# Linear attention and a two-layer MoE: fixed-scale float16 attention products, with a range flag and a float32 path behind a branch

## The chip, the cores and the metric

The kernel runs on one core of a Trainium2 chip. Its engines are TensorE (PE, matrix products, with PEld for its weight loads), VectorE (DVE), ScalarE (ACT), GpSimd (POOL) and SyncE (SP, which issues most DMAs). Each engine works its own list of instructions in order and waits for the others by semaphores. The metric is the device time of one execution in microseconds, the median of the runs.

## The reference

Inputs: q, k, v of 8 batches, 8 heads, 576 tokens and 64 numbers; w_phi, 64 by 128; the MoE's two weights, 512 by 2048 and 2048 by 512, which come as float64. The attention is linear: every token is projected to 128 features, and the products go over features.

```python
def phi(x):
    proj = np.einsum('bhsd,df->bhsf', x, w_phi)
    proj = proj - np.max(np.abs(proj), axis=-1, keepdims=True)
    return np.concatenate([np.exp(proj), np.exp(-proj)], axis=-1)
q_p, k_p = (phi(q), phi(k))
kv = np.einsum('bhsf,bhsd->bhfd', k_p, v)
z = np.sum(k_p, axis=2)
num = np.einsum('bhsf,bhfd->bhsd', q_p, kv)
den = np.einsum('bhsf,bhf->bhs', q_p, z)[..., None] + 1e-06
# x: (num / den) as 4608 tokens by 512
h = x @ w_in
g = h * (1.0 / (1.0 + np.exp(-1.702 * h)))
return (g @ w_out).astype(np.float32)
```

The inputs are normal numbers: q, k, v and w_phi with spread 0.1, then q times 8, k times 3.368 and w_phi times 3.904; the MoE's weights with spread 1/sqrt(512) and 1/sqrt(2048).

## The kernel before

**How the list is made.** The whole program is written as operations that a `Recorder` collects. Each belongs to a part with a priority; a planner goes through them by priority, with its own costs, and writes one order for every engine. `emit` (line 399, which therefore stands in every row of the profile) then issues them. There are no loops on the chip: the program is one straight list.

**Attention.** A batch is worked in four units of two heads (`attn_unit`), with 512 tokens each in the main part and the last 64 tokens of all heads in a tail. A unit loads k, q and v (`kq`, `vn`), scales k and q by powers of two taken from their own maxima (`kq_scales`), splits them into two float16 parts (`xs`), turns them by a DMA transpose (`xT`), projects them by two float16 matmuls (`ph`), and subtracts each token's largest magnitude (DVE: `sm`, then `t`). For keys the features are Exp of +t and -t (`features_k`). For queries (`features_q`) `t` is first transposed on PE, four 128-column matmuls, since the next product needs features on the partitions. Features are split into a high part, which is a second Exp with another output type (`eh`), and a rest (`el`, `elb`, on DVE). Key features times v give `kf`, a 128 by 66 matrix for each sign and head: 64 columns of values, one that sums the features (z). After a split of `kf` (`kz`, `kzs`, `kzb`) queries times these give numerator and denominator (`nf`), and `xf` is their quotient, split again into `xo` and turned by DMA into the MoE's input `x`. The first batch and one more unit work in plain float32 (`project_whole`, `exact`).

**MoE.** The weights stay on the chip, each as two float16 parts (`wbuf`), after a scale found from their squares (`weight_scales`, `wsq`) and a split (`split_weights`). Chunks of 384 token columns run over 16 blocks of 128 hidden features: `hb` collects three float16 products (high by high, high by rest, rest by high) for each quarter of the 512 inputs, ACT makes `th` by tanh, DVE makes `g` from it, ACT and DVE split it into `gh` and `gl`, and three products of 512 columns go into `ab`. The first 512 columns go in two halves of the weights, so that work can begin before all weights are there. Attention of later batches is spread between MoE chunks by the priorities; the last part of the program is MoE alone.

**Number types on PE.** A float32 matmul is two records in the profile (a transpose is one), a float16 one is one.

## Time and profile before

| | |
|---|---|
| median of 3 runs | 1081.18 us (1080.14 to 1081.76) |
| span of the profiled execution | 1079.0 us |
| PE, DVE, ACT, POOL busy | 1046.1, 851.1, 713.4, 247.1 us |
| instructions | 22925 |
| MoE alone at the end | from about 905 us of the span |
| HBM read, written | 54.59 MB, 9.44 MB |

A row of a group gives line, engine, operation, output<-input, partitions by elements, type and count, then busy time and the mean of one in ns, then idle time before it and what ended it. A row of the timeline starts with the start and the length in us. A row of a stretch gives its bounds and length, then for PE, PEld, DVE, ACT and POOL the busy time with the count, then the granted TensorE clock, the DMA share and GB/s. Means of groups include waiting inside the pipeline, so that operations in a row take less time each than their mean.

### The profile page before, as it was taken

What the parts mean: (1) busy time and instruction counts of PE and PEld (TensorE: products, weight loads), DVE (VectorE), ACT (ScalarE), POOL (GpSimd) and SP (SyncE); (2) the same over time, 40 slices, a digit from 0 to 9 for tenths busy, and PEclk for the clock granted to TensorE, in tenths of its full rate; (3) what the DMA queues carried; (4) which work ended last, traced back from release to release, by engine and by line L of the source; (5) the groups of instructions that cost most, each with busy time, mean ns of one, the idle gap of its engine ahead of it and who ended that gap; (6) DMA issues with size and microseconds to landing.
All of it is one profiled execution on the core that took longest, in us unless ns stands there. A gap on an engine that the chain in (4) does not pass through costs nothing.

```text
span 1079.0 us, 22925 instructions
## 1 busy us (share of the span) xinstructions
PE 1046.1 (97%) x8943; PEld 723.7 (67%) x8943; DVE 851.1 (79%) x1772; ACT 713.4 (66%) x1488; POOL 247.1 (23%) x320
## 2 busy tenths in 40 slices
PE   5998999999999999999999999999999999999997
PEld 3665677778766666678866666677876666577653
DVE  5879999999999997987899978987889675232323
ACT  4778797777878686875786676866687665332322
POOL 5666113331122213211223113111133112000000
PEclk9998999999999999999999999999999999999999
DMA  8956233434343443331244342432232110000101
GB/s 277 301 186 173 87 88 70 100 76 97 76 97 94 114 98 72 82 89 31 62 126 112 57 84 50 94 84 36 56 73 60 31 40 20 1 31 2 30 1 30
DMA packets 177452, 88.59 MB, mean 82 GB/s; under 512 B 143424, under 2 KB 168128, under 8 KB 177088
## 3 DMA queue, kind: packets, MB, share of 16 engines
q1 hardware_dynamic: 177184, 86.87, 32.5%
q8 instruction: 70, 1.15, 0.4%
q10 hardware_dynamic: 160, 0.26, 0.1%
q14 instruction: 38, 0.31, 0.1%
HBM read 54.59 MB, written 9.44 MB: 59 GB/s over the span
## 4 chain that ended last, share of the span: by engine, by line
PE 76%; DVE 13%; ACT 5%; issue 3%; DMA 1%; SPq 1%; POOL 0%; DVEq 0%; ACTq 0%; POOLq 0%
PE ab L399 30%; PE hb L399 29%; PE at L399 17%; DVE sm L399 2%; DVE wbuf L399 2%; DVE gl L399 1%; DVE t L399 1%; ACT e L399 1%; DVE ks L399 1%; DVE el L399 1%; DVE xs L399 1%; DVE elb L399 1%; DVE g L399 1%; SPq L399 1%; DVE vs L399 1%
## 5 line engine op out<-in xcount | busy, mean ns | idle before, releaser
L399 PE MATMUL hb<-x,wbuf 128*128 128x192 f16 (+3 forms) x3264 | 476.4, 280 | 1.2 <-DVE g L399 0.6
L399 PEld LDWEIGHTS <-wbuf 128*128 128x128 f16 (+1 forms) x3392 | 286.4, 98 | 79.9 <-issue 1.8
L399 PE MATMUL ab<-wbuf,gh 128*128 128x512 f16 x1152 | 337.9, 380 | 0.5 <-ACT gh L399 0.3
L399 ACT ACTIVATE th<-hb,usc 128x384 f32<-128x384 f32 (+1 forms) x208 | 115.8, 558 | 145.5 <-PE hb L399 142.8
L399 PE MATMUL ab<-wbuf,gl 128*128 128x512 f16 x576 | 194.1, 379 | 1.4 <-DVE gl L399 1.1
L399 DVE SCALAR_TENSOR_TENSOR g<-th,hb 128x384 f32<-128x384 f32 (+1 forms) x208 | 107.1, 516 | 95.6 <-ACT th L399 93.3
L399 PEld LDWEIGHTS <-gh 128*128 128x128 f16 x1152 | 107.7, 98 | 81.1 <-ACT gh L399 2.6
L399 ACT ACTIVATE gh<-g,al 128x384 f16<-128x384 f32 (+1 forms) x176 | 106.9, 607 | 52.6 <-DVE g L399 52.0
L399 DVE SCALAR_TENSOR_TENSOR gl<-g,al,gh 128x384 f16<-128x384 f32 (+1 forms) x176 | 109.9, 625 | 39.9 <-ACT gh L399 31.4
L399 POOL TENSOR_TENSOR xf<-nf,rc 128x512 f32<-128x512 f32 x28 | 34.2, 1220 | 410.8 <-DVE rc L399 331.3
L399 PE MATMUL at<-ph,xT 128*128 128x128 f16 x976 | 102.4, 219 | 0.0
L399 DVE TENSOR_REDUCE sm<-at 128x4 f32<-128x512 f32 x126 | 85.6, 680 | 17.8 <-PE at L399 17.4
L399 ACT ACTIVATE e<-at 128x512 f32<-128x512 f32 x144 | 85.4, 601 | 20.8 <-PE at L399 19.7
L399 ACT ACTIVATE e<-t 128x512 f32<-128x512 f32 x144 | 88.2, 630 | 11.8 <-DVE t L399 11.1
L399 DVE SCALAR_TENSOR_TENSOR t<-at,ks,sm 128x512 f32<-128x512 f32 x122 | 90.4, 743 | 1.1
L399 PEld LDWEIGHTS <-gl 128*128 128x128 f16 x576 | 54.8, 98 | 50.4 <-DVE gl L399 8.9
L399 DVE TENSOR_TENSOR el<-e,eh 128x512 f16<-128x512 f32 x108 | 75.4, 698 | 13.3 <-ACT eh L399 11.5
L399 DVE TENSOR_TENSOR elb<-e,eh 128x512 bf16<-128x512 f32 x110 | 77.9, 708 | 5.7 <-ACT eh L399 4.3
L399 PE MATMUL at<-vs,eh 128*128 128x132 f32 x216 | 81.8, 379 | 0.0
L399 PE MATMUL at<-kzs,eh 128*128 128x132 f32 x224 | 79.4, 373 | 0.8 <-ACT nf L399 0.5
L399 PEld LDWEIGHTS <-xT 128*128 128x128 f16 x976 | 69.8, 98 | 12.9 <-issue 0.3
L399 ACT ACTIVATE eh<-t 128x512 fp32r<-128x512 f32 x109 | 67.1, 635 | 1.1 <-DVE t L399 1.1
(199 smaller groups left out, 1845.6 us busy)
## 6 DMA issues: line engine op xcount, KB each, us to landing
vn<-in_v_dram SPq DMA_DIRECT2D x64, 128.0 KB, 2.7
kq<-in_k_dram SPq DMA_DIRECT2D x32, 256.0 KB, 3.2
kq<-in_q_dram SPq DMA_DIRECT2D x32, 256.0 KB, 3.0
tl<-in_v_dram SPq DMA_DIRECT2D x18, 384.0 KB, 3.2
x<-in_moe_w_in_dram SPq DMA_DIRECT2D x10, 512.0 KB, 6.0
x<-in_moe_w_out_dram SPq DMA_DIRECT2D x10, 512.0 KB, 6.3
out_dram<-osb SPq DMA_DIRECT2D x36, 128.0 KB, 2.4
out_dram<-osb SPq DMA_DIRECT2D x16, 256.0 KB, 2.5
```

The lines of the kernel that those rows point to most:

```text
L399: f(*[g(a) for a in args], **{k: g(a) for k, a in kw.items()})
```

## The change

**The fast path** (`attn_moe_fast`) takes fixed powers of two for all scales in place of maxima: `kq_scales`, `batch_max`, `weight_scales` and `split_weights` go. All attention products use float16 high and rest parts; `el` is always float16. The high part is a copy of the float32 Exp and no longer a second Exp. Copies, scalings and two-input operations may be given by the planner to one of two or three engines (`R.evac`: ACT or DVE, `R.two`: DVE or POOL, `R.three`: all), whichever is free first. The projection of queries is done twice, once by token for the maximum alone and once with features on the partitions, by two 512-column matmuls (`project_q`), in place of `t` and its transposes; the maximum then enters as a factor (`token_scales`). Only keys of batch 0 are in plain float32 (`EXK`), and batch 0 runs in phases: all keys, then the queries of half of the tokens, then of the other half.

**The flag** (`in_range`) compares the largest magnitudes of v, the weights and w_phi with bounds (`lo_hi`), the sums `akz` with 1e30 and every entry of `art` with 16. `numden` with `more` puts z, summed over all 128 features, into a column of `nt`, and `ratio` adds z times the reciprocal of the denominator (`rc`) to `art`, unit by unit. The flag is the smallest of all conditions.

**The branch.** All engines load the flag; where it is 0, `attn_moe_general` computes everything again in float32 into the same output: a loop over batches with 8 heads in its body, tiles of 96 tokens, the weights in float32, and a second loop over batches for the MoE with 6 tiles in its body.

```diff
-    def parts(b, src, e, hi, lo):
-        his, los = two(hi, b, "eh"), two(lo, b, "el")
-        for i, sg in enumerate((1.0, -1.0)):
-            R.scalar.activation(e[i], src, AF.Exp, scale=sg)
-            R.scalar.activation(his[i], src, AF.Exp, scale=sg)
-            h = his[i] if i == 0 and b else f32(his[i])
-            R.vector.tensor_sub(los[i], e[i], h)
-        return list(zip(his, los))
...
-        qt = psa()
-        e = new("e")
-        for j in range(4):
-            R.tensor.transpose(qt[:, j * P : (j + 1) * P], t[:, j], ident, also=(e,))
...
+    def features_k(t, hi="eh", lo="el"):
+        t = t.rearrange("p a f -> p (a f)")
+        pr = []
+        for sg, b in ((U, 0.0), (-U, -EK * LN2)):
+            e, h, l = new("e"), new(hi), new(lo)
+            R.scalar.activation(e, t, AF.Exp, scale=sg, bias=b)
+            R.three.copy(h, e)
+            R.two.tensor_sub(l, e, h)
+            pr.append([x.rearrange("p (a f) -> p a f", a=4) for x in (h, l)])
...
+    def project_q(xT, m, bank, also=()):
+        pp3 = by_token(xT, bank, ())
+        R.vector.tensor_reduce(m, pp3, AX.X, ALU.max, apply_absolute_value=True)
+        pT = psa()
+        mv = xT.rearrange("p t s -> p (t s)")
+        R.tensor.matmul(pT, ph[:, 0], mv, start=True, stop=False, also=also)
+        R.tensor.matmul(pT, ph[:, 1], mv, start=False, stop=True)
+        return pT
...
+    PH, VS, ONE, WS, GS = 2.0**11, 2.0**15, 2.0**4, 2.0**8, 2.0**7
...
+    EXK, EXQ = (True,) * 4, ((False,) * 4, (False,) * 4)
...
+    EK, EQ, KZ = 3, 8, 13
+    EPD = LEPS + (4 - EQ - EK - KZ) * LN2
...
+    lo_hi = [(2.0**-6, 2.0)] * B + [
+        (2.0**-8 * WS, 0.25 * WS), (2.0**-8 * WS, 8.0 * WS), (0.0, 2.0), (-1.0, 0.5), (-1.0, 0.5)
+    ]
...
+    def numden(kz, st, mv, n, c, dst, more=()):
+        nd = psa()[:, 0 : n * 2 * DV].rearrange("p (j s d) -> p j s d", j=n, s=2)
+        mm = []
+        for s in range(2):
+            for i in range(len(st)):
+                (eh, el), r = st[i][s], mv[i]
+                o = nd[:, i, s] if len(st) == n else nd[:, :, s]
+                a, z = (kz[:, x, r, s] for x in range(2))
+                mm += [(eh, a, o), (eh, z, o), (el, a, o)]
+        for w, z in more:
+            mm.append((w, z, nd[:, :, 1, D + 1]))
...
+        ratio(rc.rearrange("p (h j) -> p h j", h=2),
+              nt[:, 2 * hp : 2 * hp + 2, D + 1].unsqueeze(2).broadcast_to([P, 2, w]),
+              art[:, 0, 0:n].rearrange("p (h j) -> p h j", h=2))
...
+    def ratio(rc, z, acc):
+        r = new("rc")
+        if len(rc.t.shape) == 3:
+            r = r[:, 0 : 2 * rc.t.shape[2]].rearrange("p (h j) -> p h j", h=2)
+        R.two.tensor_mul(r, rc, z)
+        R.two.tensor_add(acc, acc, r)
...
+    def in_range():
+        s = small(16, "sc")
+        R.vector.tensor_copy(s[:, 0:B], vmx)
+        R.vector.tensor_reduce(
+            s[:, B : B + 2], wmx.rearrange("p (j t) -> p t j", t=2), AX.X, ALU.max
+        )
+        R.vector.tensor_copy(s[:, B + 2 : B + 3], phm)
+        for i, (x, lim) in enumerate(((akz, 1e30), (art.rearrange("p a j -> p (a j)"), 16.0))):
+            n = x.t.shape[-1]
+            ok = new("e")[:, 0:n]
+            R.vector.tensor_scalar(ok, x, lim, None, ALU.is_le)
+            R.vector.tensor_scalar(ok, ok, -1.0, 1.0, ALU.mult, ALU.add)
+            R.vector.tensor_reduce(s[:, B + 3 + i : B + 4 + i], ok, AX.X, ALU.max)
...
+        R.vector.tensor_tensor(ok, row, high, ALU.is_le)
+        R.vector.tensor_tensor(ok2, row, low, ALU.is_ge)
+        R.vector.tensor_mul(ok, ok, ok2)
...
+        R.vector.tensor_reduce(flag, ok, AX.X, ALU.min)
...
+    R.part(10.0, 10.0)
+    in_range()
+    R.late = (R.ops[-1], lambda: got.append(
+        nc.values_load(flag.get(), min_val=0, max_val=1,
+                       skip_runtime_bounds_check_because="a product of comparisons is 0 or 1")
+    ))
+    with tc.manual_schedule():
+        R.emit()
+    return got[0]
...
+def attn_moe_general(ctx, tc, q, k, v, w_phi, w_in, w_out, out, xd):
...
+    TS = 96
+    NS = S // TS
...
+    def turned(src, rows, cols, nm):
+        tp = ps.tile([P, 512], F32, name="gtp", tag="gtp")
+        nc.tensor.transpose(tp[0:cols, 0:rows], src, ident[0:rows, 0:rows])
+        dst = wk.tile([P, P], F32, name=nm, tag=nm)
+        nc.vector.tensor_copy(dst[0:cols, 0:rows], tp[0:cols, 0:rows])
+        return dst[0:cols, 0:rows]
+    def shifted(src):
+        xT = turned(src, TS, D, "gxT")
+        pp = ps.tile([P, 512], F32, name="gpp", tag="gpp")[0:TS, 0:NF]
+        nc.tensor.matmul(pp, xT, wp, start=True, stop=True)
+        m = wk.tile([P, 1], F32, name="gm", tag="gm")[0:TS]
+        nc.vector.tensor_reduce(m, pp, AX.X, ALU.max, apply_absolute_value=True)
+        t = wk.tile([P, NF], F32, name="gt", tag="gt")[0:TS]
+        nc.vector.tensor_scalar(t, pp, m, None, ALU.subtract)
+        return t
+    with tc.For_i(0, B) as b:
+        for h in range(H):
+            qkv = wk.tile([P, 3, NS, D + 1], F32, name="gqkv", tag="gqkv")[0:TS]
+            for i, src in enumerate((q, k, v)):
+                nc.sync.dma_start(
+                    qkv[:, i, :, 0:D],
+                    src[b, h].rearrange("(p t) d -> p t d", t=NS),
+                )
+            nc.vector.memset(qkv[:, 2, :, D : D + 1], 1.0)
+            kv = ps.tile([P, 512], F32, name="gkv", tag="gkv")
+            es = []
+            for t in range(NS):
+                u = shifted(qkv[:, 1, t, 0:D])
+                e = wk.tile([P, 2, NF], F32, name=f"ge{t}", tag=f"ge{t}")[0:TS]
+                nc.scalar.activation(e[:, 0], u, AF.Exp)
+                nc.scalar.activation(e[:, 1], u, AF.Exp, scale=-1.0)
+                es.append(e)
+            kf = wk.tile([P, 2, D + 1], F32, name="gkf", tag="gkf")
+            for s in range(2):
+                o = kv[:, s * 128 : s * 128 + D + 1]
+                for t in range(NS):
+                    nc.tensor.matmul(
+                        o, es[t][:, s], qkv[:, 2, t], start=t == 0, stop=t == NS - 1
+                    )
+                nc.vector.tensor_copy(kf[:, s], o)
+            x = wk.tile([P, NS, D], F32, name="gx", tag="gx")[0:TS]
+            for t in range(NS):
+                u = turned(shifted(qkv[:, 0, t, 0:D]), TS, NF, "guT")
+                e = wk.tile([P, 2, P], F32, name="geq", tag="geq")
+                nc.scalar.activation(e[:, 0, 0:TS], u, AF.Exp)
+                nc.scalar.activation(e[:, 1, 0:TS], u, AF.Exp, scale=-1.0)
+                nd = ps.tile([P, 512], F32, name="gpp", tag="gpp")[0:TS, 0 : D + 1]
+                for s in range(2):
+                    nc.tensor.matmul(nd, e[:, s, 0:TS], kf[:, s], start=s == 0, stop=s == 1)
+                r = wk.tile([P, 1], F32, name="gr", tag="gr")[0:TS]
+                nc.vector.tensor_scalar(r, nd[:, D : D + 1], EPS, None, ALU.add)
+                nc.vector.reciprocal(r, r)
+                nc.vector.tensor_scalar(x[:, t], nd[:, 0:D], r, None, ALU.mult)
+            nc.sync.dma_start(xd[b, h].rearrange("(p t) d -> p t d", t=NS), x)
...
+        nc.scalar.activation(dst, hi.bitcast(F32), AF.Copy, scale=2.0**-112)
+        nc.vector.scalar_tensor_tensor(dst, dst, -(2.0**32), dst, ALU.mult, ALU.max)
...
+        nc.gpsimd.tensor_scalar(lo, top, 0.9375 * 2.0**-13, 0.0, ALU.mult, ALU.add)
+        nc.vector.scalar_tensor_tensor(
+            dst.bitcast(I32), dst.bitcast(I32), 3, lo, ALU.logical_shift_left, ALU.bitwise_or
+        )
...
+    with tc.For_i(0, B) as b:
+        for t in range(NS):
+            x = wk.tile([P, H, D], F32, name="gxl", tag="gxl")[0:TS]
+            nc.sync.dma_start(
+                x, xd[b, :, t * TS : (t + 1) * TS].rearrange("h s d -> s h d")
+            )
+            xf = x.rearrange("p h d -> p (h d)")
+            xT = [turned(xf[:, c * P : (c + 1) * P], TS, P, f"gxT{c}") for c in range(NCT)]
+            acc = ps.tile([P, 512], F32, name="gkv", tag="gkv")[0:TS]
+            for j in range(NJ):
+                hp = ps.tile([P, 512], F32, name="gpp", tag="gpp")[:, 0:TS]
+                for c in range(NCT):
+                    nc.tensor.matmul(
+                        hp, w1[:, c, j * P : (j + 1) * P], xT[c], start=c == 0, stop=c == NCT - 1
+                    )
+                th = wk.tile([P, TS], F32, name="gth", tag="gth")
+                nc.scalar.activation(th, hp, AF.Tanh, scale=0.851)
+                g = wk.tile([P, TS], F32, name="gg", tag="gg")
+                nc.vector.scalar_tensor_tensor(g, th, 1.0, hp, ALU.add, ALU.mult)
+                nc.tensor.matmul(acc, g, w2[:, j], start=j == 0, stop=j == NJ - 1)
+            o = wk.tile([P, DM], F32, name="go", tag="go")[0:TS]
+            nc.vector.tensor_scalar(o, acc, 0.5, None, ALU.mult)
+            nc.sync.dma_start(o4[b, t], o)
...
+def attn_moe_kernel(ctx, tc, q, k, v, w_phi, w_in, w_out, out):
+    B, H, S, _ = q.shape
+    dp = ctx.enter_context(tc.tile_pool(name="gd", bufs=1, space=bass.MemoryType.DRAM))
+    xd = dp.tile([B, H, S, D], F32, name="gxd")
+    ok = attn_moe_fast(tc, q, k, v, w_phi, w_in, w_out, out)
+    with tc.If(ok == 0):
+        attn_moe_general(tc, q, k, v, w_phi, w_in, w_out, out, xd)
```

First place: the query and key operations of the fast path on VectorE, in the part where attention and MoE run together. Names: `sm` and `mq` are maxima, `t` the shifted projection, `el` and `elb` rests of features. Before, a query's maximum is followed by a scaling and by `t`:

```order
L399 TENSOR_SCALAR sm_129<-sm_127,ks_85 128x4
L399 TENSOR_REDUCE sm_130<-at_62 128x4
L399 RECIPROCAL rc_138<-rc_138 128x8
L399 TENSOR_SCALAR sm_128<-sm_130,ks_76 128x4
L399 SCALAR_TENSOR_TENSOR g_115<-th_113,hb_65 128x256
L399 SCALAR_TENSOR_TENSOR t_91<-at_62,ks_76,sm_128 128x512
```

And of the change, where a query's maximum `mq` stands alone and the sum of numerators comes as additional operations:

```order
L458 TENSOR_REDUCE mq_147<-at_65 128x4
L458 TENSOR_REDUCE wmx_224<-w_231 128x1
L458 TENSOR_TENSOR n_118<-n_118,cs_153 128x198
L458 TENSOR_TENSOR n_119<-n_119,cs_153 128x132
L458 TENSOR_TENSOR nf_121<-at_64,n_118 128x198
L458 TENSOR_TENSOR nf_121<-at_66,n_119 128x132
```

The pass `t` over 512 elements is gone for queries, and passes over 132 and 198 elements (`n`) and the weights' maxima (`wmx`) stand between.

Second place: VectorE behind the branch, one query tile of the float32 path in the loop over batches (of the change only; `gtp`, `gpp` are PSUM banks, `guT` the transposed features' argument, `gxT` the transposed input of a later tile, `gm` its maximum, `gr` the reciprocal of the denominator, `gx` the result).

```order
L1286 COPY guT<-gtp 128x96
L1286 COPY gxT<-gtp 64x96
L1294 TENSOR_REDUCE gm<-gpp 96x1
L1334 TENSOR_SCALAR gr<-gpp 96x1
L1296 TENSOR_SCALAR gt<-gpp,gm 96x128
L1335 RECIPROCAL gr<-gr 96x1
L1336 TENSOR_SCALAR gx<-gpp,gr 96x64
```

The same query tile on TensorE, in the same loop:

```order
L1284 MATMUL gtp<-gident,gt 128x96
L1284 MATMUL gtp<-gident,gqkv 64x96
L1332 MATMUL gpp<-gkf,geq 96x65
L1292 MATMUL gpp<-gphi,gxT 96x128
L1332 MATMUL gpp<-gkf,geq 96x65
```

None of these rows has a counterpart before: there the program ends with the MoE's last products.

Third place: TensorE in the second loop, a pair of hidden blocks of the float32 MoE (`gw_15877` and `gw_15878` are the float32 weights, `gg` the activated hidden block).

```order
L1379 MATMUL gpp<-gxT_16087,gw_15877 128x96
L1379 MATMUL gpp<-gxT_16091,gw_15877 128x96
L1379 MATMUL gpp<-gxT_16095,gw_15877 128x96
L1379 MATMUL gpp<-gxT_16099,gw_15877 128x96
L1379 MATMUL gpp<-gxT_16087,gw_15877 128x96
L1379 MATMUL gpp<-gxT_16091,gw_15877 128x96
L1379 MATMUL gpp<-gxT_16095,gw_15877 128x96
L1379 MATMUL gpp<-gxT_16099,gw_15877 128x96
L1386 MATMUL gkv<-gw_15878,gg 96x512 x2
```

Eight products of 96 columns fill two banks, then two of 512 columns take both hidden blocks.

More of the change, by code (lines that the diff above doesn't have):

```diff
@@ L1 @@
-from contextlib import ExitStack
+import math
 import concourse.bass as bass
@@ L25 @@
 EPS = 1e-6
+LN2 = math.log(2.0)
+LEPS = math.log(EPS)
 class _Buf:
@@ L621, in split_weights @@
-    def split_weights(j):
-        for t in range(2):
-            i = 2 * j + t
-            sc = sw[:, half(j), t : t + 1]
-            R.scalar.activation(w16[:, i, 0], wbuf[:, i + 1], AF.Copy, scale=sc)
-            R.vector.scalar_tensor_tensor(
-                w16[:, i, 1], wbuf[:, i + 1], sc, w16[:, i, 0], ALU.mult, ALU.subtract
-            )
+            if not WIDE:
+                R.two.tensor_scalar(y, y, WS, 1.0, ALU.mult, ALU.mult)
+            R.three.copy(w16[:, i, 0], y)
+            R.two.tensor_sub(w16[:, i, 1], y, w16[:, i, 0])
@@ new lines, in turned_back, with queries @@
+    def turned_back(xj, hp, x16, g):
+        tp = psa()[:, 0 : 2 * P]
+        for j in range(2):
+            R.tensor.transpose(tp[:, j * P : (j + 1) * P], xj[:, j], ident)
+        s = slice(2 * P * g, 2 * P * g + 2 * P)
+        R.evac.copy(x16[:, 0, hp, s], tp)
+        R.vector.tensor_sub(x16[:, 1, hp, s], tp, x16[:, 0, hp, s])
+    def queries(hp, qt_, kz, nt, x16, bank, g=None):
+        n = 8 if g is None else 4
+        w = n // 2
+        nf = new("nf")[:, 0:n]
+        xT = turned(qt_, g)
+        m = new("mq")[:, 0:n]
+        eq = [
+            features_q(project_q(xT[:, h : h + 4], m[:, h : h + 4], bank, (nf,)))
+            for h in range(0, n, 4)
+        ]
+        cs = token_scales(m, n)
+        for s0, c in ((0, 3), (3, 3), (6, 2)) if g is None else ((0, 2), (2, 2)):
+            sl = range(s0, s0 + c)
+            numden(
+                kz,
+                [[[e[:, x % 4 * P : x % 4 * P + P] for e in eq[x // 4][s]] for s in range(2)]
+                 for x in sl],
+                [x // w for x in sl],
+                c,
+                cs[:, 0, s0 : s0 + c],
+                nf[:, s0 : s0 + c],
+            )
+        rc = new("rc")[:, 0:n]
+        R.two.tensor_add(rc, nf[:, :, D], cs[:, 1])
+        R.vector.reciprocal(rc, rc)
+        xj = divided(nf, rc, w)
+        if g is not None:
+            turned_back(xj, hp, x16, g)
@@ L1224, in attention @@
-        R.part(u + 0.003 if b == 0 else u - 0.01, u)
-        tl = tail_load(b)
-        def bank():
-            return R.tile(ab, whole=True) if b == 0 else psa()
+        xs[b] = (x16[:, 0], x16[:, 1])
+        return x16
+    def attention(b):
+        u = v_att(4 * b)
+        x16 = place(b)
+        R.part(u - 0.01, u)
+        tl = tail_load(b)
+        nt = new("nt")
+        R.part(u, u + 0.266)
+        tail = attn_tail(b, tl, psa)
+        for hp in range(NHP):
+            w = v_att(4 * b + hp)
+            R.part(w, w + 0.517)
+            kt, qt, vn = attn_load(b, hp)
+            kf, kz = keys(b, hp, kt, vn, tail, nt, False, False, psa)
+            queries(hp, qt, kz, nt, x16, psa)
+            if hp == NHP - 1:
+                queries_tail(nt, tail[3], x16)
@@ L1265, in attn_moe_kernel @@
             moe_chunk(0, c, 256, part_)
+    for i in range(NBLK):
+        R.part(3.0 + 0.2 * i, 3.0 + 0.2 * i, after=250e3)
+        weight_max(i)
     for sb in range(B // SB):
```

954 lines of the change are left out of this document (420 added, 534 removed), and 25 rows, old and new, of the table PLACES.

## The prediction

> **What bounds the kernel now.** I read the page's head and chain first, then the stretches, then the forms of instructions.
>
> ```profile
> span 1079.0 us, 22925 instructions
> PE 1046.1 (97%) x8943; PEld 723.7 (67%) x8943; DVE 851.1 (79%) x1772; ACT 713.4 (66%) x1488; POOL 247.1 (23%) x320
> PE 76%; DVE 13%; ACT 5%; issue 3%; DMA 1%; SPq 1%; POOL 0%; DVEq 0%; ACTq 0%; POOLq 0%
> ...
> 162.00:216.00 54.00, 52.64 (x518) 39.42 (x516) 53.77 (x129) 42.04 (x100) 17.20 (x21) 1.00 0.39 85
> 324.00:378.00 54.00, 53.98 (x471) 36.12 (x470) 53.97 (x122) 40.24 (x87) 14.69 (x19) 1.00 0.42 104
> ...
> 905.00:1073.00 168.00, 167.98 (x1116) 101.70 (x1115) 54.49 (x96) 59.18 (x103) 5.17 (x6) 1.00 0.04 12
> ```
>
> In the stretches, the columns behind the length are the busy time of PE, PEld, DVE, ACT and POOL, then the granted clock. PE is busy 97% of the span. From 162 to 378 us DVE is as full as PE (53.77 of 54 us, 53.97 of 54); the last 168 us are MoE alone, with PE at 167.98. So a cut on PE in the first half helps only as far as DVE is cut too. Span and median differ by 1081.18 - 1079.0 = 2.2 us, which I add at the end.
>
> **The step that decides: which way the branch goes.** The fast path now sets a flag, and the float32 path runs behind it when the flag is 0. One of its conditions is that `art` stays at or below 16 in every slot. `art` is a sum: `ratio` adds z * rc to it in every unit, so each slot of the main tokens gets 8 batches * 4 pairs = 32 terms, all positive. A term is z/den. Its scales: query features are exp(-p) * 2^-8, z is the sum of the key features over 128 features with ones as weights, so z/den is 2^8 divided by the weighted mean of exp(-p) (the second sum of den only adds a little to den). The reference draws q with a spread of 0.1 * 8 and w_phi with 0.1 * 3.904, so p has a spread of 0.8 * 0.39 * sqrt(64) = 2.5, the mean of exp(-p) is about exp(2.5^2/2) = 23, and a term is about 256/23 = 11. Thirty-two of them make some 350. Worked through with the reference's own inputs and the formulas of the diff, the median term is 15.6 and the 512 sums (128 partitions, 4 token groups of the natural layout) lie between 395 and 806. The limit is 16; no rounding closes a factor of 25. The other conditions hold (largest |v| 0.49, |w_in| 0.22 below its 0.25, |w_phi| 1.42 below 2), but the flag is a minimum over all. So I expect flag 0, and the time is the fast path plus the whole float32 path, one behind the other.
>
> **The fast path** is bounded, not worked out to a microsecond, since it is a quarter of the sum.
>
> ```profile
> L399 DVE SCALAR_TENSOR_TENSOR t<-at,ks,sm 128x512 f32<-128x512 f32 x122 | 90.4, 743 | 1.1
> L399 PE MATMUL at<-ident,t 128*128 128x128 f32 x288 | 46.6, 274 | 2.8 <-DVE t L399 1.8 <-ACT t L399 0.9
> L399 PE MATMUL at<-e,kf 128*66 128x512 f32 x40 | 18.2, 595 | 0.3 <-ACT kf L399 0.2
> ...
> 33.12 0.60 PE L399 MATMUL at<-ident,t 128*128 128x128 f32 x4
> 31.40 1.88 PE L399 MATMUL at<-e,kf 128*66 128x512 f32 x4
> 35.40 1.02 PE L399 MATMUL at<-e,kf 128*66 128x512 f32 x2
> ...
> L399 POOL TENSOR_TENSOR xf<-nf,rc 128x512 f32<-128x512 f32 x28 | 34.2, 1220 | 410.8 <-DVE rc L399 331.3
> ```
>
> PE loses the 288 transposes of t, at (0.60 - 0.27)/3 = 0.11 us each 31 us, and the 40 records e,kf at (1.88 - 1.02)/2 = 0.43 us, 17 us; the two 512-column matmuls that replace the transposes give back about 6 us and the third float16 product some 3. That is about -39 us: were PE the bound all the way, the span would be 1040. On DVE about half of the t pass goes (the queries', some 45 us), but the splits of features and keys (sub on DVE or POOL, since the second Exp became a copy) and 32 maxima over the weights come in, and POOL, at 1.22 us for a 512-wide pass with two inputs, gets more of them. The stretch from 108 to 400 us, where DVE is full, therefore gives back most of it; were POOL's added passes to hold DVE up beyond that, by 25 us more than is saved, the span would be 1095, an estimate for the other side (some 50 more two-input passes of 1.22 us, of which half a microsecond each falls on DVE). I take 1070, between the two and near the span of before. The flag's own operations and the load of it on five engines lie some us before MoE's end and beside it: nothing; without that cover under 3 us.
>
> **The float32 path, attention.** A loop over 8 batches, in its body 8 heads of 6 key tiles and 6 query tiles of 96 tokens. The rows that price its steps:
>
> ```profile
> 6.97 0.29 DVE L399 TENSOR_REDUCE sc<-wst 128x1 f32<-128x128 f32 x1 [6.97 <-DMA wst<-in_w_phi_dram]
> 7.40 0.37 PE L399 MATMUL at<-ident,sc 128*1 128x128 f32 x1 [7.40 <-DVE sc L399]
> 7.82 0.28 DVE L399 TENSOR_REDUCE sc<-at 1x1 f32<-1x128 f32 x1
> 8.13 0.32 DVE L399 TENSOR_SCALAR sc<-sc 1x1 int32<-1x1 int32 x2
> 8.50 0.58 PE L399 MATMUL at<-sc,ones 1*128 1x1 f32 x2 [0.72 <-DVE sc L399]
> ...
> L399 DVE TENSOR_TENSOR nf<-at,lq 128x132 f32<-128x132 f32 x27 | 7.7, 286 | 0.6 <-ACT lq L399 0.6
> L399 DVE TENSOR_SCALAR rc<-nf 128x8 f32<-128x8 f32 x28 | 4.5, 162 | 0.1
> L399 ACT COPY ls<-at 128x128 f32<-128x128 f32 x54 | 14.0, 259 | 19.9 <-PE at L399 19.8
> 11.47 0.40 ACT L399 ACTIVATE ph<-wst,phs 128x128 f16<-128x128 f32 x1 [0.96 <-DVE phs L399]
> ...
> 34.92 0.65 PE L399 MATMUL ab<-wb,t 128*128 128x256 f32 x2
> ...
> vn<-in_v_dram SPq DMA_DIRECT2D x64, 128.0 KB, 2.7
> ```
>
> One query tile is a ring, since each engine works in order: transpose of gt (PE), copy guT (DVE), exp (ACT), first num/den matmul and then the next tile's projection (PE), its maximum gm, gr of this tile, gt (DVE), and the next transpose. Step by step: DVE to PE and a single transpose 0.14 + 0.37 = 0.51; to DVE 0.05 and a copy of 96 columns 0.25 (below the 0.286 for 132); to ACT and 96 columns of Exp 0.35 (between 0.259 and 0.40); to PE 0.05, one small float32 matmul of two passes 0.58 (the row at 8.50) and the streaming of 65 and 128 columns, twice each at 0.00084 us a column (0.43 for 512; the row wb,t has 0.65 for two passes of 256, 0.43 of streaming and 0.2 of way), 0.3: 0.9; maximum 0.05 + 0.29; gr 0.16; gt 0.25. Sum 2.8 us, six times 16.8. Key tiles run without that ring: copy 0.25, maximum 0.29, subtract 0.25 on DVE and 0.2 for waits, six of them 6.0; the last Exp pair, the second six products (two passes of 65 columns each, 0.11) and the copy of gkf, 1.9. A head: 24.7 us; 64 heads 1581. Loads (two buffers) are hidden, since one lands in 2.7 us. Each of the 8 turns of the loop drains all engines and waits for a store and a load again: 8 us each, an estimate from landings of 3 us twice and a first tile, 64. Bounds: if DVE's own work alone set the pace (1.5 us a query tile, 0.8 a key tile) 14 us a head, 900; at 0.15 us for each hand-over and PE passes twice as long, 31 us a head, 1990.
>
> **The weights**, 32 blocks through two buffers:
>
> ```profile
> L399 POOL TENSOR_SCALAR x<-x 128x512 int32<-128x512 uint16 x20 | 34.2, 1711 | 2.3 <-DMA x<-in_moe_w_in_dram 0.9
> L399 DVE SCALAR_TENSOR_TENSOR wbuf<-wbuf,x 128x512 int32<-128x512 int32 x20 | 14.7, 752 | 0.4 <-POOL x L399 0.4
> L399 ACT ACTIVATE wbuf<-x 128x512 f32<-128x512 f32 x20 | 13.4, 678 | 0.0
> x<-in_moe_w_in_dram SPq DMA_DIRECT2D x10, 512.0 KB, 6.0
> ```
>
> Landing 5, ACT 0.68, POOL 1.6, DVE 0.75: 8 us for a buffer, 4 a block, 128 in all; from 51 (POOL alone) to 290 (nothing beside anything).
>
> **The float32 MoE**, 48 tiles of 96 tokens, 16 blocks of 128 hidden features each. In the program's order PE takes two blocks at a time: 8 matmuls of 96 columns into two banks, then 2 of 512. By 0.86 us for 512 columns (40 records stand for 20 matmuls, two of 0.43 us each) these are 8 * 0.16 + 2 * 0.86 = 3.0 us. The first of the 512-wide ones waits for tanh and the product of its block: 0.05 + 0.27 + 0.05 + 0.28 + weights 0.25 = 0.9 us after its bank, of which the second bank's 0.65 covers most: 0.3. A pair 3.3, a tile of 8 pairs 26.4, 48 tiles 1267, with the tiles' ends 1290; from 1160 (no wait) to 1540 (4.0 a pair, weight loads not hidden). Eight turns of the loop at 9 us: 72.
>
> **Sum.** 1070 + 2.2 + 1581 + 64 + 128 + 1290 + 72 = 4207; the first instructions behind the branch add little. I say **4200 us**, 3.9 times the time before.
>
> **A lower clock.** PE works about a quarter of the attention loop (6.7 us of streaming a head by the rates above).
>
> ```profile
> 0.00:10.00 10.00, 0.95 (x3) 0.57 (x3) 1.38 (x8) 1.61 (x2) 8.41 (x31) 1.00 0.50 128
> 81.00:108.00 27.00, 22.21 (x166) 14.97 (x164) 25.29 (x45) 21.84 (x44) 18.68 (x17) 0.87 0.63 174
> ```
>
> The granted clock is 1.00 in the first 10 us with PE busy for 0.95 of them, and 0.87 where PE was busy for 22 of 27 us: busy time alone does not set it here. With half the clock a query tile's ring would get 0.04 + 0.11 + 0.22 us longer and streaming elsewhere as much again: about 4.4 us a head, 280 in all, 4490 us. The Trainium skill's "TensorE: Matmul & The Clock Gate", section "Part 1: The HAM clock gate (the "warmup" mystery)", has a half-rate state after an idle window of about 3.4 us and a full one after a busy window; its Part 4 adds that transposes do not count as busy. By that rule gaps of 1 to 2 us, shorter than the window, would not throttle by themselves, while a loop of thin work and transposes could; the first row disagrees with it, and no row here settles it.
>
> **Rivals.** (1) The flag is 1 after all, because I misread a scale by 2^5 or more, or because the branch is not taken: then only the fast path counts, 1040 to 1097 us, likeliest 1072: not slower, or within a few per cent. It decides at one point: every `art` slot at or below 16. Against it stand the sums from 395; for it only that I could err in six scale factors. Chance 0.05. (2) The clock halves in the loop: 4490. The first of the two rows above speaks against it (1.00 with PE nearly idle), the second for it (0.87 beside gaps). Chance 0.2. (3) The engines run further apart than my rings say (the order lets PE take the next head's first key tiles during the last query tiles) and the head is DVE's own work plus little: 17 us a head, 64 * 7.7 = 490 less, 3710. For it: DVE's tiny rows are 0.13 to 0.16. Against: four of the five DVE steps of a query tile wait for the one before. Chance 0.2. (4) The forecast, 4200 with its own spread of about 250: 0.55.
>
> **How the numbers follow.** Range 3500 to 5100: rivals 2 and 3 lie inside; the ends are where two of the large terms (attention 900 to 1990, MoE 1160 to 1540) come near the same bound together; about 0.12 lies outside, rival 1 among it. A measurement of this kernel tells 0.2% (2 us) from no change. Of rival 1's 0.05, 0.025 is faster, 0.005 the same, 0.02 slower; everything else is slower: 0.97.
>
> **What would show it.** Right: a profile of several ms with lines of the float32 path (gpp, gkv, geq) in the groups, a first part of about 1070 us that looks like before, then 8 equal turns of some 205 us with PE below a third, some 130 us with POOL first, and 8 turns of some 170 us with PE over 85%. Wrong: a span near 1070 with no such line. A turn of 250 us or a clock of 0.5 there speaks for rival 2, one of 140 for rival 3.

## The result and the profile after

The changed kernel takes 4757.64 us, median of 4 runs (4752.46 to 4761.23), against 1080.91 us before in the same runs: 4.40 times as long, with a 95% interval of 4.394 to 4.407. The prediction was 4200 us with 3500 to 5100. The flag came out 0, and both paths run, one behind the other. The span of the profiled execution is 4754.2 us.

The head of the page after, with the busy shares of PE and DVE and the granted clock in 40 slices of 119 us:

```profile
span 4754.2 us, 63844 instructions
...
PE 4030.0 (85%) x23554; PEld 2699.6 (57%) x23554; DVE 2042.3 (43%) x6676; ACT 1174.9 (25%) x3686; POOL 393.6 (8%) x533
...
PE   6898899998878788787878787863999999999999
...
DVE  8999937733444444444444444443111111111111
...
PEclk8999999998555555555555555556999999999999
```

Four stages can be told apart: some ten slices like before, a loop with DVE at 4 and the clock at 0.5, one slice with PE low, and twelve with PE full. PE's own timeline (start, length, engine, line, operation; in brackets the idle time before and what ended it) gives the bounds to the microsecond:

```profile
1137.40 0.38 PE L458 MATMUL ab<-w,gl 128*128 128x512 f16 x1
1150.75 0.50 PE L1284 MATMUL gtp<-gident,gqkv 96*64 96x96 f32 x2 [12.97 <-DMA gqkv<-in_v_dram]
...
3179.08 0.90 PE L1332 MATMUL gpp<-gkf,geq 128*96 128x65 f32 x4 [0.73 <-ACT geq L1328]
3279.12 0.58 PE L1284 MATMUL gtp<-gident,gxl 96*128 96x96 f32 x2 [99.14 <-DMA gxl<-gxd]
```

| stage | forecast | measured | difference |
|---|---|---|---|
| fast path, to the first float32 product | 1070 | 1150.75 | +81 |
| float32 attention, to 3179.98 | 1581 + 64 | 2029 | +384 |
| float32 weights | 128 | 99 | -29 |
| float32 MoE, to the span's end | 1290 + 72 | 1475 | +113 |
| median less span | 2.2 | 3.4 | +1 |
| sum | 4207 | 4757.6 | +550 |

Of the first 81 us, 12.97 are PE's wait for the first load behind the branch, in the second row. The largest error is in the attention loop. One query tile there, all engines but PE's weight loads, in the timeline after:

```profile
1519.58 0.42 PE L1284 MATMUL gtp<-gident,gt 96*128 96x96 f32 x1 [0.51 <-DVE gt L1296]
...
1520.11 0.26 DVE L1286 COPY guT<-gtp 128x96 f32<-128x96 f32 x1 [0.20 <-PE gtp L1284]
...
1520.40 0.28 ACT L1328 ACTIVATE geq<-guT 128x96 f32<-128x96 f32 x1 [2.97 <-DVE guT L1286]
...
1520.73 0.58 PE L1332 MATMUL gpp<-gkf,geq 128*96 128x65 f32 x2 [0.57 <-ACT geq L1328]
...
1521.25 0.74 PE L1292 MATMUL gpp<-gphi,gxT 64*96 64x128 f32 x2
...
1521.91 0.58 PE L1332 MATMUL gpp<-gkf,geq 128*96 128x65 f32 x2
1522.02 0.29 DVE L1294 TENSOR_REDUCE gm<-gpp 96x1 f32<-96x128 f32 x1 [1.50 <-PE gpp L1292]
1522.53 0.15 DVE L1334 TENSOR_SCALAR gr<-gpp 96x1 f32<-96x1 f32 x1 [0.22 <-PE gpp L1332]
1522.61 0.34 DVE L1296 TENSOR_SCALAR gt<-gpp,gm 96x128 f32<-96x128 f32 x1
...
1523.00 0.42 PE L1284 MATMUL gtp<-gident,gt 96*128 96x96 f32 x1 [0.51 <-DVE gt L1296]
```

The ring has the steps that the prediction drew, in its order. It takes 1523.00 - 1519.58 = 3.42 us and not 2.8. Most of the extra lies at PE: from the first product with `geq` to the end of the projection it is 1.26 us (1520.73 to 1521.99) where the forecast had 0.9 with the way to PE, and the second product then ends so late (1522.49) that `gr` waits 0.22 us for it after the maximum, a wait the forecast did not have. The other steps differ by less than 0.1 us each.

### The profile page after: what moved, and what is told of

Read it like the earlier page. It is cut to its first block, busy times and chain, and to the rows that moved or that the text cites. A ratio compares the mean times of both kernels' runs of the same rounds, so it can differ in the third digit from the quotient of the medians.

```text
span 4754.2 us, 63844 instructions
## 1 busy us (share of the span) xinstructions
PE 4030.0 (85%) x23554; PEld 2699.6 (57%) x23554; DVE 2042.3 (43%) x6676; ACT 1174.9 (25%) x3686; POOL 393.6 (8%) x533
## 5 line engine op out<-in xcount | busy, mean ns | idle before, releaser
L1379 PEld LDWEIGHTS gpp<-gxT,gw 128*128 128x128 f32 x6144 | 762.5, 195 | 178.2 <-issue 177.1
L1379 PE MATMUL gpp<-gxT,gw 128*128 128x96 f32 x6144 | 757.5, 277 | 0.0
L1386 PE MATMUL gkv<-gw,gg 128*96 128x512 f32 x1536 | 740.7, 605 | 7.0 <-DVE gg L1385 7.0
L1332 PE MATMUL gpp<-gkf,geq 128*96 128x65 f32 x1536 | 440.5, 390 | 148.3 <-ACT geq L1328 148.3
L1292 PE MATMUL gpp<-gphi,gxT 64*96 64x128 f32 x1536 | 547.4, 467 | 3.3 <-DVE gxT L1286 3.3
L1332 PEld LDWEIGHTS gpp<-gkf,geq 128*96 128x96 f32 x1536 | 304.6, 259 | 344.5 <-ACT geq L1328 238.7
L458 PE MATMUL hb<-x,w 128*128 128x192 f16 (+3 forms) x3264 | 452.1, 280 | 7.7 <-DVE g L458 6.3
L1320 PE MATMUL gkv<-gqkv,ge 96*128 96x65 f32 x1536 | 424.1, 430 | 20.3 <-ACT ge L1313 20.3
L1320 PEld LDWEIGHTS gkv<-gqkv,ge 96*128 96x128 f32 x1536 | 355.8, 322 | 116.1 <-ACT ge L1313 50.8
L458 PE MATMUL ab<-w,gh 128*128 128x512 f16 x1152 | 325.7, 382 | 4.4 <-ACT x L458 3.2
```

The lines of the kernel that those rows point to most:

```text
L458: f(*[g(a) for a in o.args], **{k: g(a) for k, a in o.kw.items()})
L1292: nc.tensor.matmul(pp, xT, wp, start=True, stop=True)
L1320: nc.tensor.matmul(o, es[t][:, s], qkv[:, 2, t], start=t == 0, stop=t == NS - 1)
L1332: nc.tensor.matmul(nd, e[:, s, 0:TS], kf[:, s], start=s == 0, stop=s == 1)
L1379: nc.tensor.matmul(hp, w1[:, c, j * P : (j + 1) * P], xT[c], start=c == 0, stop=c == NCT - 1)
L1386: nc.tensor.matmul(acc, g, w2[:, j], start=j == 0, stop=j == NJ - 1)
```

## The experiments

Twelve kernels ran: two take the paths apart, three read the clock, one asks what a narrow float32 pass costs, and six look for what the fast path lost. Times are medians; the ratio is to the kernel before, measured beside it, with its 95% interval.

### The branch, and the two paths apart

f1_limit_open lets `art` be anything, so that the float32 path is not entered:

```diff
-        for i, (x, lim) in enumerate(((akz, 1e30), (art.rearrange("p a j -> p (a j)"), 16.0))):
+        for i, (x, lim) in enumerate(((akz, 1e30), (art.rearrange("p a j -> p (a j)"), 1e30))):
```

> The limit on art is 1e30 in place of 16; nothing else is changed, so all work of the fast path and the branch stay. Theory (art alone sends the program into the float32 path, and the fast path is slower than before by itself): 1140 to 1155 us, no rows of lines above 1260. Rival 1 (another condition fails too): 4757 as before. Rival 2 (the fast path is as forecast and the rest of its 1143 us in the trace is a hand-over to the branch): 1070 to 1100.

Measured: 1151.31 us (1150.16 to 1153.22), ratio 1.064 [1.0625, 1.0661]. So `art` alone sends the kernel into the branch, and the fast path by itself is already 6.4% slower than the kernel before.

g0_float32_alone computes the float32 path only and leaves the fast path out:

```diff
-    ok = attn_moe_fast(tc, q, k, v, w_phi, w_in, w_out, out)
-    with tc.If(ok == 0):
-        attn_moe_general(tc, q, k, v, w_phi, w_in, w_out, out, xd)
+    attn_moe_general(tc, q, k, v, w_phi, w_in, w_out, out, xd)
```

> Only the float32 path, without the fast path and the branch. Theory (the two run one behind the other): 4757 less the fast path's 1143, 3600 to 3630 us, with the granted clock at 0.50 in the attention loop and above 0.9 in the MoE loop as in the changed kernel. Rival (the state that the fast path leaves matters, a clock that was set down there or output stores in the way): under 3400.

Measured: 3601.4 us. With f1's 1151.3 that is 4752.7, 5 us from the 4757.6 of both: the paths add up, nothing overlaps, and the branch itself costs next to nothing. One thing did not fit. The group of the projection in g0:

```profile
L1292 PE MATMUL gpp<-gphi,gxT 64*96 64x128 f32 x1536 | 547.4, 467 | 3.3 <-DVE gxT L1286 3.3
```

A stretch of g0's attention loop (bounds and length, busy time of PE, PEld, DVE, ACT and POOL, then the granted clock):

```profile
400.00:1400.00 1000.00, 784.06 (x2822) 530.88 (x2822) 435.94 (x1983) 177.76 (x752) 0.00 (x0) 1.00 0.08 19
```

On the page of the changed kernel the same group has the same row, figure for figure. A stretch of its loop:

```profile
1400.00:2900.00 1500.00, 1180.27 (x4250) 800.78 (x4250) 655.08 (x2976) 267.48 (x1134) 0.00 (x0) 0.50 0.08 19
```

The mean is 467 ns in both, yet the clock's record says 1.00 in one and 0.50 in the other. One of the two records is wrong, and the clock has to be read from lengths of instructions instead.

### The clock, read from lengths

Three kernels, g1_pe_filled_1, g2_pe_filled_2 and g3_pe_filled_8, put one, two or eight float16 products of 384 columns behind every transpose of g0. Their results go to unused columns of the same bank.

```diff
+    wz = cp.tile([P, 512], F16, name="gwz")
+    nc.vector.memset(wz, 0.0)
...
         nc.tensor.transpose(tp[0:cols, 0:rows], src, ident[0:rows, 0:rows])
+        for _ in range(8):
+            nc.tensor.matmul(tp[:, P:512], wz[:, 0:P], wz[:, P:512], start=True, stop=True)
```

> As g0; behind each transpose PE gets one more float16 product of 384 columns into unused columns of the same bank, which nothing reads; on the query tile's ring two of these fall into the 0.57 us in which PE waits for Exp. Theory (the low clock, which follows from PE's thin work, lengthens the ring): if they lift the clock to 1.0 the query tile goes from 3.42 to about 2.9 us and the whole to about 3300; if the clock stays at 0.50, the ring stays at 3.4 to 3.8 us and the whole at 3600 to 3800. Rival (hand-overs between engines set the ring, not the clock): no run with a higher clock is shorter than g0.

> As g1 with two such products behind each transpose. Theory: clock 1.0 and a query tile of 2.9 to 3.1 us, the whole 3300 to 3400 (four products of 0.16 us are 0.07 us more than the gap). With the clock still at 0.50 the four take 1.28 us and the ring grows to 4.1 us: 3950. Rival as in g1.

> As g1 with eight products of 384 columns behind each transpose, so that PE streams for most of the attention loop. It is longer by their length; what counts is the length of single steps. Theory (PE's rate halves when its array is mostly idle; the granted clock of 1.00 that g0 and g1 record in this loop is a value that was never updated): at least in part of the loop a product of 384 columns takes 0.16 us and not the 0.32 of g1, and the projection of 128 columns in two passes about 0.45 us and not 0.74. Rival (these lengths are what such instructions take at any load): 0.32 and 0.74 throughout.

Measured: 3827.97, 3892.16 and 4751.05 us (two runs, two and one). The first is longer than either of its forecasts, the second lies below the 3950 us of a half rate throughout, and the third met its theory on the lengths, as follows. PE's timeline in the second, in a query tile:

```profile
499.50 0.53 PE L1288 MATMUL gtp<-gwz 128*128 128x384 f16 x1
...
502.51 0.85 PE L1288 MATMUL gtp<-gwz 128*128 128x384 f16 x2
```

and in the third, in a query tile too:

```profile
504.04 0.46 PE L1296 MATMUL gpp<-gphi,gxT 64*96 64x128 f32 x2 [0.34 <-DVE gxT L1290]
505.35 0.27 PE L1286 MATMUL gtp<-gident,gt 96*128 96x96 f32 x1 [0.85 <-DVE gt L1300]
505.45 1.47 PE L1288 MATMUL gtp<-gwz 128*128 128x384 f16 x8
...
506.84 0.81 PE L1288 MATMUL gtp<-gwz 128*128 128x384 f16 x4
```

A second product behind the first adds 0.85 - 0.53 = 0.32 us with two in a row, and a further one (1.47 - 0.81)/4 = 0.165 us with eight. The fast path has the full rate on record: 21 products of the same size in a row, in the timeline after:

```profile
1130.31 3.58 PE L458 MATMUL hb<-x,w 128*128 128x384 f16 x21
```

That is about 0.17 each. The kernel with two products has both rates inside a head. PE's timeline in its key tiles and at the second set behind them, and then two stretches, one mostly of key tiles and one of query tiles:

```profile
444.74 0.49 PE L1288 MATMUL gtp<-gwz 128*128 128x384 f16 x2
...
445.15 0.33 PE L1288 MATMUL gtp<-gwz 128*128 128x384 f16 x1
...
449.81 2.79 PE L1324 MATMUL gkv<-gqkv,ge 96*128 96x65 f32 x12
```

```profile
440.00:450.00 10.00, 9.88 (x52) 6.55 (x51) 6.22 (x25) 3.29 (x14) 0.00 (x0) 0.84 0.05 16
460.00:470.00 10.00, 8.79 (x30) 4.89 (x30) 3.67 (x17) 1.20 (x6) 0.00 (x0) 0.50 0.01 2
```

In the key tiles, where PE has next to no idle time (9.88 of 10 us busy), the second product adds 0.49 - 0.33 = 0.16 us; in the query tiles it is 0.32, and here the record of the clock agrees with the lengths. So in the changed kernel's loop PE really worked at half its rate, and it reached the full rate only where it was given more work. At the full rate the loop's own products are shorter too: the projection's two passes 0.46 us instead of 0.74, the transpose 0.27 instead of 0.42, and the second set of `gkv`, here in the changed kernel (with four passes of the first set before it) and then in g3:

```profile
1537.21 1.11 PE L1320 MATMUL gkv<-gqkv,ge 96*128 96x65 f32 x4
...
1538.64 2.82 PE L1320 MATMUL gkv<-gqkv,ge 96*128 96x65 f32 x12
```

```profile
442.35 1.55 PE L1324 MATMUL gkv<-gqkv,ge 96*128 96x65 f32 x12
```

From these rows the price of the half rate can be estimated. A query tile: two passes of the first product 0.26 us less (half of the 0.52 from their start to the projection's), the projection 0.28, the transpose 0.15, and the 0.22 that `gr` waits: 0.9 us, times 384 tiles, 346 us. The second set: 1.27 us, times 64 heads, 81. Together some 430 us, against a miss of 384: at the full rate the loop would have come out near the forecast's 1645. That stays an estimate, and one by the half rate alone: no run has the loop as it is at the full rate, since g3 pays for its filling with more time than it wins (4751 against 3601 us).

### What a narrow float32 pass costs

g4_moe_32_columns is g0 where three of the four products of each hidden block cover 32 tokens instead of 96; the hidden blocks lack the rest.

```diff
-                        hp, w1[:, c, j * P : (j + 1) * P], xT[c], start=c == 0, stop=c == NCT - 1
+                        hp[:, 0 : TS if c == 0 else 32], w1[:, c, j * P : (j + 1) * P],
+                        xT[c][:, 0 : TS if c == 0 else 32], start=c == 0, stop=c == NCT - 1
```

> The float32 path alone (g0_float32_alone, 3601 us) where of the four products of every hidden block (each two passes) the last three cover only 32 of the 96 tokens, so that streaming falls from 96 to 32 columns in three quarters of the passes; the weights they load are the same 128 columns. The MoE's hidden blocks are therefore not the reference's. Theory 'the passes of 96 columns go at the pace of their weight loads' (0.12 us a pass after, against 0.081 that my prediction took from streaming): the 16 passes of a pair stay at about 1.75 to 1.9 us and the whole at 3570 to 3605. Rival 'streaming at 96 columns sets the pace': 12 of 16 passes cost a third, a pair falls by 12 * 0.08 = 0.96 us, 384 pairs by 370 us: about 3230.

Measured: 3634.52 us, one run. PE's timeline in the changed kernel (96 columns throughout):

```profile
3403.93 1.92 PE L1379 MATMUL gpp<-gxT,gw 128*128 128x96 f32 x16
3405.69 1.89 PE L1386 MATMUL gkv<-gw,gg 128*96 128x512 f32 x4
3407.41 1.92 PE L1379 MATMUL gpp<-gxT,gw 128*128 128x96 f32 x16
...
3410.90 1.36 PE L1379 MATMUL gpp<-gxT,gw 128*128 128x96 f32 x11
```

and in g4 (a row shows the first record's shape; 12 of 16 passes have 32 columns):

```profile
2164.40 3.46 PE L1379 MATMUL gpp<-gxT,gw 128*128 128x96 f32 x16
...
2605.19 1.87 PE L1379 MATMUL gpp<-gxT,gw 128*128 128x96 f32 x16
...
2608.67 1.53 PE L1379 MATMUL gpp<-gxT,gw 128*128 128x96 f32 x13
```

A pass costs (1.92 - 1.36)/5 = 0.112 us with 96 columns and (1.87 - 1.53)/3 = 0.113 with mostly 32. So the columns streamed do not set the pace here, and the rival, 3230 us, falls. What all 16 passes share is the load of 128 float32 weight columns, and two rows shown above bear out that it sets the pace. In the attention loop, at half the rate, a pass with 96 weight columns takes (0.90 - 0.58)/2 = 0.16 us (`geq`, at 3179.08 and at 1520.73) and one with 128 takes (2.82 - 1.11)/8 = 0.21 (`ge`, at 1537.21 and 1538.64), both with 65 columns streamed: as 96 to 128. The Trainium skill, "TensorE: Matmul & The Clock Gate", section "LDWEIGHTS (loading the stationary operand)", prices a load in nanoseconds at its columns over 1.2, 107 ns for 128; the 0.112 and 0.113 us agree.

The whole was 3634 and not 3570 to 3605. The first row of g4 says why: at 2164 us the same 16 records took 3.46 us, twice as long. In g0 each of the MoE loop's eight turns begins with some 10 us of such rows; in g4 they last from 2126 to 2200 us in the first turn and from 3254 to 3303 in the seventh, and up to some 15 us in the others. Half the rate over some 110 us more than in g0 costs about 55, an estimate; the 0.05 us that a group of 16 is shorter (1.92 to 1.87) gives back 19 in 384 groups. The measured difference from g0 is 33.

### Where the fast path lost 70 us

All of these are f1 with one or two more edits. f2_pool_two_input_to_dve issues POOL's additions, subtractions and products on DVE, at the same place in the order:

```diff
-            f = getattr(getattr(self.nc, o.eng), o.meth)
+            eng = o.eng
+            if eng == "gpsimd" and o.meth in ("tensor_sub", "tensor_mul", "tensor_add"):
+                eng = "vector"
+            f = getattr(getattr(self.nc, eng), o.meth)
```

> As f1, and every subtraction, product and sum that the planner gave to POOL is issued on DVE at the same place of the order (some 100 passes of 512 elements, 58 of 132 or 198, small ones). Theory (DVE and POOL hold each other up): DVE takes on about 90 us of passes at 0.6 us, and loses most of its 140 us above its undisturbed sum, so DVE busy stays within 820 to 860 us and the time within 1130 to 1160. Rival (DVE is full and POOL's help is worth its length): the 90 us come on top, 1200 to 1240.

f3_no_checks leaves out the sums `akz` and `art` (every operation that writes them, and `ratio`'s product), and puts a constant for the weights' maxima `wmx`, so that the flag no longer depends on them:

```diff
+            tl = getattr(o.args[0], "tl", None)
+            if tl in self.drop and o.meth != "memset":
+                continue
+            if tl is not None and tl is self.fill:
+                self.nc.vector.memset(g(o.args[0]), 30.0)
+                continue
...
+    R.drop |= {akz.tl, art.tl}
+    R.fill = wmx.tl
...
+        R.drop.add(r.tl)
```

> As f1, without what the flag is made of: no sums akz and art, and the 32 maxima of the weights are memsets of one column. Theory (these lie in the stretch where DVE is full): DVE loses 18 us of maxima, 12 of akz and what collides with POOL's 37 us of akz, art and products; 1095 to 1120 us. Rival (they lie beside other work, as the prediction had it): within 5 us of f1.

f4_both has both edits.

> f2 and f3 together. Theory: the two gains add, within 10 us of f2 + f3 - f1, and about 1085 to 1110 if collisions weigh as much as the moved work. Rival (DVE full by work): above 1160.

p1_no_table takes the table of priorities away, so that the priorities in the calls stand; p0_no_table_no_checks_dve does so on f4:

```diff
-PLACES = (
-    (-1000.000, -1000.000), (10.366, 36.856), (-103.145, -96.665), (-88.176, -77.356), (-98.560, -83.513),
...
+PLACES = ()
```

> As f1 (limit on art open), with the table of priorities (PLACES) empty, so that the planner uses the priorities written beside each part; the same operations. By the order of PE's matmuls, attention is then 70% issued when 52% of the MoE's matmuls are, against 38% in f1 and 54% in the kernel before. Theory (the table packs attention, and so DVE's work, into the first 594 us, where DVE is full and PE idles, and leaves DVE idle later): PE's idle time between 54 and 594 us falls from 80 us to under 45, and the time to 1085 to 1125. Rival (DVE has too much work whatever the order): within 15 us of 1151.

> As f4 (no checks, POOL's two-input work on DVE) with the empty table. Theory: f4's 16 us below f1 come on top of the order's gain, 1070 to 1110, which would be about as fast as before. Rival (moving POOL's work to DVE costs where DVE is not full all the time): above p1.

f5_copies_to_act issues every copy that the planner gave to DVE, and that ACT could do, on ACT:

```diff
+            eng, meth = o.eng, o.meth
+            if eng == "vector" and meth == "tensor_copy" and any(x[0] == "scalar" for x in o.alts):
+                eng, meth = "scalar", "copy"
```

> f1_limit_open (1151.3 us) with one thing changed: every plain copy that the planner had given to DVE although ACT could do it (42 high parts of features of 476 ns, and some 40 others; about 36 us of DVE busy time in all) is issued on ACT instead, at the same place in the program's order. Theory 'DVE sets the pace from 54 to 594 us, ACT has room there (170 and 180 of 270 us busy)': some two thirds of those 36 us lie in that stretch, so 1125 to 1138. Rival 'ACT's order is itself in the chain' (an in-order ACT now holds exponentials and tanh up behind copies of 0.62 us): 1148 to 1165. DVE's busy time should fall from 846 to about 810 in either case. In the float32 path nothing is said by this run, since it isn't entered.

| kernel | us | ratio | DVE, POOL busy | against f1 |
|---|---|---|---|---|
| f1 | 1151.31 | 1.064 [1.0625, 1.0661] | 845.8, 373.2 | |
| f2, POOL's two-input work on DVE | 1153.39 | 1.067 [1.0649, 1.0690] | 858.6, 125.2 | +2 |
| f3, no checks | 1141.09 | 1.055 [1.0533, 1.0568] | 812.1, 332.8 | -10 |
| f4, both | 1135.39 | 1.050 [1.0475, 1.0533] | 824.3, 122.7 | -16 |
| p1, no table | 1143.14 | 1.057 [1.0549, 1.0587] | 855.2, 314.1 | -8 |
| p0, no table on f4 | 1134.91 | 1.049 [1.0474, 1.0509] | 836.7, 116.4 | -16 |
| f5, copies on ACT | 1143.57 | 1.058 [1.0536, 1.0614] | 816.4, 367.3 | -8 |

Of the six, only f2 came out inside what its theory expected. f4 met one half of its own: the gains of f2 and f3 add to within 10 us (1143.2 by the sum), but it is not at 1085 to 1110. p1 met its rival, within 15 us of 1151: with the table away PE idled 66 us from 54 to 594 us, not under 45. f3, p0 and f5 fell between theory and rival; f5's DVE came down to 816 us where 810 was expected.

The costliest group of DVE in f1 and then in f2 says what POOL's help was worth:

```profile
L458 DVE TENSOR_TENSOR el<-e,eh 128x512 f16<-128x512 f32 x183 | 153.7, 859 | 3.1 <-PE at L458 1.5 <-ACT eh L458 0.6
```

```profile
L461 DVE TENSOR_TENSOR el<-e,eh 128x512 f16<-128x512 f32 x240 | 165.2, 707 | 1.9 <-PE at L461 0.7 <-ACT eh L461 0.4
```

With 57 subtractions more, DVE's busy time in this group rose by only 11.5 us, because each became shorter by 0.15 us; on POOL the 57 had taken 76.9 us. Over the whole kernel POOL's busy time fell by 248 us and DVE's rose by 13. Beside POOL's two-input work DVE's own is held up by nearly as much as POOL takes off it. The Trainium skill, "SBUF — State Buffer", section "Who interferes with whom", says that a DVE instruction with two inputs in SBUF and a GpSimd instruction that reads SBUF exclude each other; f2 agrees, and gives the size that it has here.

Where the time goes is seen in the stretches. Before:

```profile
54.00:324.00 270.00, 258.97 (x2442) 190.06 (x2440) 257.96 (x563) 212.12 (x462) 86.04 (x94) 0.99 0.42 105
324.00:594.00 270.00, 269.91 (x2448) 190.20 (x2447) 245.52 (x525) 196.47 (x416) 65.08 (x90) 1.00 0.37 88
```

f1:

```profile
54.00:324.00 270.00, 221.69 (x2476) 152.87 (x2476) 254.38 (x470) 169.86 (x408) 143.01 (x173) 0.94 0.46 105
324.00:594.00 270.00, 237.80 (x2843) 155.18 (x2840) 260.60 (x473) 179.56 (x412) 144.11 (x170) 0.99 0.39 86
594.00:864.00 270.00, 262.56 (x2295) 168.49 (x2294) 156.27 (x296) 115.08 (x249) 41.65 (x56) 1.00 0.19 43
```

and f4:

```profile
54.00:324.00 270.00, 230.84 (x2567) 157.30 (x2567) 247.03 (x563) 174.56 (x415) 46.41 (x51) 0.94 0.44 105
324.00:594.00 270.00, 243.68 (x2904) 159.22 (x2902) 259.10 (x559) 184.25 (x421) 37.75 (x47) 1.00 0.41 90
```

From 54 to 594 us PE was busy 528.9 of 540 us before and 459.5 in f1: 69 us, about as much as the fast path lost. DVE is at 515 of 540 there and at 156 of 270 behind it. ACT had room (349 of 540), but sending it DVE's copies bought 8 us for 29 us less on DVE. No kernel tried moves more than 16 of the 70 us; with the best of them 54 stay. What it is in the first 594 us, the phases of batch 0 or DVE's chain from the exponential to the rest part, is open: the phases were not undone by themselves. The granted clock is a third candidate: from 54 to 324 us it is recorded as 0.94 in f1 and f4 and as 0.99 before. If that record is right, f1's PE ran at half its rate for some 30 of these 270 us, an estimate; whether that adds to the loss or only follows from PE's idle time, no run here separates. No version came near 1081 us.

## Why the prediction came out as it did

**The branch: right.** That `art` exceeds 16 decided the sign and three quarters of the time, and f1 and g0 show it: without that condition 1151 us, the float32 path 3601 more.

**The fast path: a term mis-sized, outside its bounds.** It took 1151 us against 1070 and bounds of 1040 to 1095. Of the 39 us that PE was to lose, 14.5 are in the record (1046.1 to 1031.6 busy). The step "POOL's added passes to hold DVE up", with its half microsecond for each of some 50 passes, had the mechanism right, as f2 shows. What the bound left out is PE's idle time: span less busy is 120 us in f1 (1151.5 - 1031.6) and 33 before. What causes the larger part of it stays open, as said above. The checks had no price of their own beside their maxima; the sums and maxima cost 10 us (f3).

**The attention loop: right ring, wrong rate.** The step that failed is "A lower clock", where the prediction held the first row, clock 1.00 with PE nearly idle, against a half rate. g0 shows a record of 1.00 over a stretch that ran at half the rate, so that row carried no weight; g2 and g3 show the rate by lengths. Rival 2 is what happened, and its sign, a turn of 250 us, is met: 2029/8 = 254. Its price, 280 us, was too low, because it doubled only the streaming: a pass in the loop with 128 weight columns takes 0.21 us, as worked out above, where the forecast had 0.055 for 65 columns streamed, 0.11 at half the clock.

"PE below a third" was wrong for the same reason: by the record PE is busy 1180 of 1500 us, since its passes last several times what their streaming was priced at. The trace and the rule that the prediction cited, the Trainium skill's "TensorE: Matmul & The Clock Gate", "Part 1: The HAM clock gate (the "warmup" mystery)" (half rate after an idle window of about 3.4 us), disagree if only gaps count: the ring's gaps on PE are near 0.5 us (0.51 and 0.57 in the rows above). The 12.97 us without work ahead of the loop could have started the half rate by that rule; but in g2 it sets in with no gap on PE, at 449.81, where twelve passes take 2.79 us against 1.55 at the full rate. With its caveat in the same part, that recorded clock events on trn2 have been seen to be unreliable, g0 agrees.

**The weights: over-priced.** POOL's pass was taken at 1.6 us, from a row of 1.71 in the kernel before; here it takes 0.66, with DVE busy for only 43.6 of the 94 us from 3185 to 3279. That the lighter load on DVE is the reason is argued and was not tried. The landing of 5 us stood in no row (6.0 in the one shown); the loads here land in 3.5 to 3.8. The group in the changed kernel:

```profile
L1354 POOL TENSOR_SCALAR graw<-graw 128x512 int32<-128x512 uint16 x32 | 21.1, 658 | 2114.9 <-DMA gxd<-gx 2040.1 <-DMA graw<-in_moe_w_in_dram 37.2 <-DMA graw<-in_moe_w_out_dram 36.3
```

POOL waits 37.2 + 36.3 us of the 99 for the loads, so that landings are the larger part of a buffer's turn, as the forecast had it; the turn is 99/16 = 6.2 us and not 8.

**The MoE: mechanism right, passes mis-sized.** A pair takes 3407.41 - 3403.93 = 3.48 us against 3.3: the passes go at 0.112 us, the weight load, and not at the 0.081 that half of 0.16 for a matmul implied (g4). Two errors partly cancel in the 3.3: the passes take 3405.69 - 3403.93 = 1.76 us where 8 * 0.16 = 1.28 was added, and the wait of 0.3 for the hidden block is not there; PE's products of 512 columns waited 7.0 us for `gg` in the whole run:

```profile
L1386 PE MATMUL gkv<-gw,gg 128*96 128x512 f32 x1536 | 740.7, 605 | 7.0 <-DVE gg L1385 7.0
```

Over 384 pairs the net 0.18 us is 70 of the 113 us; the rest are ends of tiles and turns, 17 us a turn (1475/8 - 48 * 3.48) instead of 12. Some 3 of the 17 are the half rate that opens every turn (an estimate from the rows at the end of this document).

The forecast's own spread of 250 us was too narrow, then. No price that the prediction named comes to 4758 us, not even rival 2's 4490; the wider range held the time because it kept both ends of the two large terms. That is width, and in part luck: the weights and the wait in a pair were over-priced while nearly everything else was under-priced.

## What to carry to other kernels

Check a guard's limit against the sum it guards with the real inputs: one comparison chose between 1151 and 4757 us. Price a narrow float32 product by its weight load, not by its columns, and in a loop of thin dependent products, as here, reckon with PE at half its rate until lengths of instructions say otherwise. Two-input work that is handed to GpSimd beside a full VectorE may be worth nothing: here 77 us of it on GpSimd relieved VectorE of 11.5.
